# Eight attention groups that load their keys once for two groups

## The chip, the cores and the metric

The kernel runs on one core of one Trainium2 chip. The metric is the device time of a run in microseconds (us), taken as the median of three runs. Five engines work side by side, each through its own row of instructions in order: TensorE (PE: matrix products, with PEld for the loading of its stationary operand), VectorE (DVE), ScalarE (ACT), GpSimd (POOL) and SyncE (SP, which here issues the DMAs). An instruction that needs another engine's result waits for a semaphore, and everything behind it in the same row waits too.

## The reference

Three stages follow each other, on float32 data. Attention has 4 batches, 8 heads, 576 positions and 64 numbers per head; a position sees itself and the 63 before it:

```python
scores = scale * np.matmul(q, k.transpose(0, 1, 3, 2))
mask = (rel >= 0) & (rel < window)          # window = 64
scores = np.where(mask, scores, -1000000000.0)
attn = np.exp(scores - np.max(scores, axis=-1, keepdims=True))
attn = attn / (np.sum(attn, axis=-1, keepdims=True) + 1e-09)
return np.matmul(attn, v)
```

Its output, 2304 rows of 512, goes through `softplus(x @ w_in) @ w_out` (512 to 2048 to 512), and that through `(sigmoid(x @ w_gate) * (x @ w_val)) @ w_out` (512 to 1536 to 512). The result is 2304 x 512.

## The kernel before, in words

**Groups.** Attention is cut into 36 groups of 64 query positions, nine to a batch (`NSEQ`). One group does all 8 heads as 4 pairs (`NPAIR`). Its queries stand block-diagonally, so that one product gives two heads: 128 rows of queries (two heads of 64) against the keys of that pair. The window makes a group need two blocks of 64 keys, its own and the one before; the first group of a batch needs only its own. The input `qk[g]` holds for each group the queries (`qk[g, :, 0]`, 256 KB) and both key blocks (`qk[g, :, 1]`, 256 KB), so each key block lies in memory twice, once for each group that uses it.

**The lead-in.** The tokens of the first big product are cut into blocks (`BLOCKS1`), the first of 512 tokens. That block needs eight groups (`NG0`, groups 0 to 7), and these are worked off before anything else, in the stretch that this document calls the lead-in. Later groups are computed between the products and are not touched by the change. A group of the lead-in goes through these steps, one function each:

- `qk_load`, `v_load` (SP): its queries and keys, its values.
- `att_scores` (PE, L286 and L289): a product of an identity with a mask opens the PSUM bank, then four products, one for each pair of heads, add the scores to it.
- `att_max` (DVE, L299): the maximum of each row. `att_exp` (ACT, L314 and L316): one small scaling, then four exponentials that also sum up their rows. `att_sum` (DVE, L322 and L325): adds the sums and takes the reciprocal. `att_norm` (POOL, L330): multiplies by it.
- `att_transpose` (PE, L338), `att_copy` (DVE or ACT, L367), `att_values` (PE, L376): the probabilities are turned, copied out of PSUM and multiplied with the values.
- `att_hi` (ACT, L384) and `att_lo` (DVE, L389): the result is split into a high and a low part and stored in `xt`, the input of the first big product.

The scores of group g go to the PSUM bank `acc0`, `acc1` or `h1` by g modulo 3. Beside this, the first weights are unpacked (`w_scale` on ACT, L160, then DVE, L179 and L187).

**The start of the main part.** The first big product (`m1_proj(0, 0)`, L394 to L396) waits for the last `att_lo` and for its weights. In front of it stand 21 products on a constant tile (`warm`, L406), which belong to no result. Six more of these open the program. From that product on PE works without long breaks to the end.

**Order.** The order of the lead-in isn't written out. A function `lead_in` plans it: each step has a due time, an engine, an assumed duration and the steps that it waits for (`traits`), and the planner takes the steps one by one by these. An `att_scores` of the lead-in is assumed to take 1.2 us on PE, a `qk_load` is a transfer of 512 KB. What it decides is the order on each engine; the chip then runs this order, whatever the real durations are.

Of the kernel before, what the change touches and what calls it, by code (L numbers as in the profile page):

```python
# [9 lines left out]
F32 = mybir.dt.float32  # L10
# [9 lines left out]
P = 128  # L20
# [21 lines left out]
def tile_kernel(ctx: ExitStack, tc: tile.TileContext, qk, vt, w1, w2, wg, wv, wo, out):  # L42
# [20 lines left out]
    nc = tc.nc  # L63
# [3 lines left out]
    Q = P // 2  # L67
# [48 lines left out]
    def pair(slot, turn, dtype, *shape):  # L116
        key = slot // 2, turn
        if key not in pair_t:
            pair_t[key] = wpool.tile([P, 2, *shape], dtype, tag=f"w{slot // 2}", name=f"w{slot // 2}", bufs=1)
        return pair_t[key]  # L120
# [147 lines left out]

    def qk_load(g):
        if g < NG0:  # L270
            t = pair(NSLOT - NG0 + g, -1, F32, 2, NPAIR, P)[:, g % 2]
        else:
            t = late["apool"].tile([P, 2, NPAIR, P], F32, tag="qk", name="qk", bufs=2)
        nc.sync.dma_start(out=t, in_=qk[g])
        qk_t[g] = t

    def near_bank(g):
# [3 lines left out]
    def att_scores(g):  # L281
        w = width(g)
        t = qk_t[g]
        s = psum(near_bank(g), 1, (P, NPAIR, P)) if g < NG0 else psum("at", 2, (P, NPAIR, P))
        if g < NG0:
            nc.tensor.matmul(out=s[:, :, :w], lhsT=ident16,  # L286
                             rhs=mask16[:, P - w:].unsqueeze(1).to_broadcast([P, NPAIR, w]), start=True, stop=False)
        for j in range(NPAIR):
            nc.tensor.matmul(out=s[:, j, :w], lhsT=t[:, 0, j, :], rhs=t[:, 1, j, :w], start=g >= NG0,  # L289
                             stop=g >= NG0 or j == NPAIR - 1)  # L290
        s_t[g] = s

    def att_max(g):
# [490 lines left out]
    def traits(fn, a, *rest):  # L784
# [3 lines left out]
        if fn is w_load:  # L788
            freed, deps, f = (w_low, a), [], (a - NSLOT) // 2
            if a >= WO_AT:  # L790
                freed, deps = (w_low, a + 1), [(c_hi, NF2 - 1, "x")]
            elif a >= NSLOT:
                freed, deps = (c_send, f, "v"), [(c_hi, f - 1, "x") if f else (w_load, NSLOT - 1)]
            u = a // 2
            slot = raw_slot(u)
            if slot and 4 <= u < 8:
                deps += [(att_scores, 2 * slot - 24), (att_scores, 2 * slot - 23)]
            elif slot and u >= 8:
                deps += [(w_low, 2 * u - 8)]
            return "sp", 512, deps + [(w_load, a - 1, None)] * (a > 0), [("raw", RB, freed)] * (  # L800
                a % 2 == 0 and slot is None)
        if fn in (qk_load, v_load):
            ring = ("qk", 2, (att_scores, a)) if fn is qk_load else ("v", VB, (att_values, a))
            return "sp", 512 if fn is qk_load else 256, [], [ring] * (not early)
        if fn is att_scores:
            if early:
                return "pe", 1.2, [(qk_load, a)], [(near_bank(a), 1, (att_exp, a))]
            return "pe", 0.9, [(qk_load, a), turned(a - 2)], [("at", 2, (att_max, a))]
        if fn is att_max:
            return "dve", 0.8 if early else 1.42 * wide, [(att_scores, a)], [("st", 4, (att_norm, a))] + [  # L810
# [29 lines left out]
        if fn is w_scale:  # L840
            deps, ring, u = [(w_load, a + k) for k in range(size(a))], [], a // 2
            if 0 < u < 4:
                deps += [(att_copy if u == 1 else att_hi, NG0 - 1)]
            if a == 1:
                deps += [(w_scale, 0), (att_copy, NG0 - 1)]
            elif u < 3:
                ring = [("g", GB, (w_lo, 2 * u + 1))]
            elif 4 <= u < 8:
                deps += [(att_scores, 4 + 2 * (u % 4 // 2)), (att_scores, 5 + 2 * (u % 4 // 2))]
            elif 8 <= u < 14:  # L850
                old = u // 2 * 2 - 4 if u < 12 else 10
                deps += [(w_lo, 2 * old + k) for k in range(4)]
            else:
                last = (c_lo, u - NSLOT // 2, "s4") if NSLOT <= a < WO_AT else (w_lo, a + size(a) - 1)
                ring = [("bits", 1, last)]
            return "act", 0.12 + 0.48 * size(a), deps, ring
# [85 lines left out]
    def lead_in():  # L942
# [29 lines left out]
        while todo:  # L972
            ready, other = [], "soft" if table == "exp" else "exp"
            for n, key in enumerate(todo[:AHEAD]):
                rank, kind, us, _, taken = nodes[key]
                deps = deps_of[key] + [rings[name][-bufs] for name, bufs, _ in taken if len(rings[name]) >= bufs]
                if all(d in done for d in deps + after[key]):
                    begin, best = max([done[d] for d in deps], default=0.0), None
                    if kind == "pe" and key[0] not in (m1_proj, m1_out) and key[1] >= NG0:
                        begin += LATE  # L980
                    for kind, us in kind if kind in CHOICES else ((kind, us),):
                        engine, *need = kind.split()
                        start = max(free[engine], begin)
                        if engine == "pool" or "lock" in need:
                            start = max(start, held["dve" if engine == "pool" else "pool"])
                        if engine == "sp" and len(flying) >= FLYING:
                            start = max(start, flying[-FLYING])
                        if engine == "act" and need and need[0] != table:
                            us += SWITCH
                        if best is None or start + us < best[0] + best[2]:  # L990
                            best = start, kind, us
                    ready.append((best[0], rank + FLIP * (best[1].split()[-1] == other), n, key, *best[1:]))
            soonest = min(r[0] for r in ready)
            start, _, n, key, kind, us = min((r for r in ready if r[0] < soonest + (NEAR if soonest < OPEN else SLACK)), key=lambda r: r[1:])
            engine, *need = kind.split()
            for name, _, freed in nodes[key][4]:
                rings[name].append(freed)
            if engine == "sp":
                free[engine] = start + 0.43
                dma = max(start + 1.3, dma) + us / 400  # L1000
                flying.append(dma + 0.75)
                done[key] = dma + 0.85 + MARGIN
            else:
                free[engine] = start + us
                done[key] = start + us + 0.08
                if engine == "pool" or "lock" in need:
                    held[engine] = start + us
                if engine == "act" and need:
                    table = need[0]
            order.append((start, len(order), key + (engine,) * (nodes[key][1] in CHOICES)))  # L1010
            del todo[n]
# [63 lines left out]
```

## Time and profile before

| what | value |
|---|---|
| median of three runs | 894.87 us (894.82 to 895.06) |
| the profiled execution | 895.09 us |
| its span, first to last instruction | 893.3 us |
| PE busy | 885.0 us, 99% of the span |
| lead-in: start of the first big product | 31.18 us after the span's start |
| traffic | 177.58 MB, on average 199 GB/s |

The span is what the rows of a profile cover; the execution lasts 1.8 us longer than it. In a row of the timeline the first number is the start, the second the time from the start of the first to the end of the last instruction in it. Ends of matrix products are modelled, so the distance from one start to the next says more than the second number. A product in float32 appears as two passes, so four products of a group are "x8". A bracket at a row's end is idle time of the engine ahead of it and what ended it.

### The profile page before, as it was taken

To read this page: it belongs to the slowest core of one execution; us is meant where nothing else is said; L and a number is where in the kernel's file an instruction comes from. 1 tells how busy PE (TensorE), PEld (TensorE's weight loads), DVE (VectorE), ACT (ScalarE), POOL (GpSimd) and SP (SyncE) were. 2 spreads that over 40 slices of the span, in tenths; PEclk is the share of its full clock that TensorE was granted. 3 is DMA by queue.
4 is the path that set the end of the run, shared out by engine and by line. 5 is a ranking of instruction groups with operands and counts; after the bars stand their busy time and mean duration, and the time that the engine had idled before them with its cause. 6 is when DMAs were issued, how large, how long until landed. Compare 5 with 4: busy or idle time off the path is not lost.

```text
span 893.3 us, 13510 instructions
## 1 busy us (share of the span) xinstructions
PE 885.0 (99%) x5035; PEld 797.6 (89%) x5035; DVE 523.8 (59%) x921; ACT 400.0 (45%) x892; POOL 153.8 (17%) x157
## 2 busy tenths in 40 slices
PE   9999999999999999999999999999999999999997
PEld 7788789999999888888889999999999999999996
DVE  4898876556555756455515667668445447444444
ACT  6867857546764755345323333334222125222222
POOL 4001102102110220002001333331111112111110
PEclk9999999999999999999999999999999999999999
DMA  9946346766885764683307565545454445544441
GB/s 349 397 151 210 134 163 210 246 199 226 270 268 205 243 234 165 209 287 130 130 1 256 220 254 203 208 174 216 179 209 159 159 164 209 183 165 165 165 165 72
DMA packets 56210, 177.58 MB, mean 199 GB/s; under 512 B 6096, under 2 KB 21456, under 8 KB 51536
## 3 DMA queue, kind: packets, MB, share of 16 engines
q1 hardware_dynamic: 56000, 176.58, 56.0%
q8 instruction: 40, 0.66, 0.3%
q14 instruction: 26, 0.21, 0.1%
q10 hardware_dynamic: 144, 0.13, 0.0%
HBM read 139.72 MB, written 36.96 MB: 198 GB/s over the span
## 4 chain that ended last, share of the span: by engine, by line
PE 97%; DVE 1%; ACT 1%; POOL 0%; issue 0%; POOLq 0%
PE h L394 17%; PE h L396 17%; PE h L395 17%; PE acc L394 11%; PE acc L395 11%; PE acc L396 11%; PE at L289 3%; PE at L376 2%; PE at L396 2%; PE at L395 2%; PE at L394 2%; PE acc L289 1%; PE h L406 1%; PE acc L338 0%; POOL w L330 0%; PE at L338 0%
## 5 line engine op out<-in xcount | busy, mean ns | idle before, releaser
L512 DVE TENSOR_TENSOR w<-h,w 128x384 f32<-128x384 f32 x216 | 117.0, 556 | 159.7 <-PE h L396 157.0
L394 PE MATMUL h<-w,wc 128*128 128x384 f32 x504 | 169.0, 335 | 0.1
L396 PE MATMUL h<-w,wc 128*128 128x384 f32 x504 | 169.0, 335 | 0.0
L395 PE MATMUL h<-w,wc 128*128 128x384 f32 x504 | 168.8, 335 | 0.0
L524 POOL TENSOR_TENSOR g<-w,g 128x384 fp32r<-128x384 f32 x70 | 74.0, 1057 | 296.7 <-ACT g L517 252.1
L394 PE MATMUL acc<-g,w 128*128 128x512 f32 (+1 forms) x320 | 119.5, 374 | 0.0
L394 PE MATMUL h<-xt,w 128*128 128x512 f32 (+1 forms) x320 | 119.4, 373 | 0.1
L396 PE MATMUL h<-xt,w 128*128 128x512 f32 (+1 forms) x320 | 117.9, 368 | 1.0 <-DVE w L187 1.0
L396 PE MATMUL acc<-g,w 128*128 128x512 f32 (+1 forms) x320 | 117.7, 368 | 0.0
L395 PE MATMUL acc<-g,w 128*128 128x512 f32 (+1 forms) x320 | 117.6, 368 | 0.0
L395 PE MATMUL h<-xt,w 128*128 128x512 f32 (+1 forms) x320 | 117.6, 368 | 0.0
L436 DVE TENSOR_TENSOR g<-h,g 128x512 fp32r<-128x512 f32 (+1 forms) x80 | 50.7, 634 | 84.1 <-ACT g L430 83.8
L394 PEld LDWEIGHTS h<-w,wc 128*128 128x128 f32 x504 | 94.6, 188 | 2.4 <-DVE w L512 0.4
L395 PEld LDWEIGHTS h<-w,wc 128*128 128x128 f32 x504 | 94.6, 188 | 2.0
L396 PEld LDWEIGHTS h<-w,wc 128*128 128x128 f32 x504 | 94.6, 188 | 0.0
L423 ACT ACTIVATE h<-h 128x512 f32<-128x512 f32 (+1 forms) x80 | 43.2, 540 | 108.7 <-PE h L396 108.3
L517 ACT CAST g<-w 128x384 fp32r<-128x384 f32 x72 | 36.9, 513 | 117.5 <-DVE w L512 117.5
L396 PEld LDWEIGHTS h<-xt,w 128*128 128x128 f32 x320 | 60.1, 188 | 9.2 <-DVE w L187 1.7
L394 PEld LDWEIGHTS h<-xt,w 128*128 128x128 f32 x320 | 60.1, 188 | 8.4 <-issue 0.6
L394 PEld LDWEIGHTS acc<-g,w 128*128 128x128 f32 x320 | 60.1, 188 | 8.0
L396 PEld LDWEIGHTS acc<-g,w 128*128 128x128 f32 x320 | 60.1, 188 | 7.6
L330 POOL TENSOR_TENSOR p<-p,st 128x512 f32<-128x512 f32 (+1 forms) x28 | 27.8, 996 | 226.2 <-DVE st L325 165.2
(129 smaller groups left out, 1440.9 us busy)
## 6 DMA issues: line engine op xcount, KB each, us to landing
wc<-wcd SPq DMA_DIRECT2D x36, 1792.0 KB, 7.3
qk<-in_qk SPq DMA_DIRECT2D x28, 512.0 KB, 5.1
wcd<-raw SPq DMA_DIRECT2D x24, 512.0 KB, 3.5
w<-in_w SPq DMA_DIRECT2D x16, 512.0 KB, 9.6
raw<-in_w SPq DMA_DIRECT2D x16, 512.0 KB, 4.6
v<-in_vt SPq DMA_DIRECT2D x25, 256.0 KB, 3.8
raw<-in_wg SPq DMA_DIRECT2D x12, 512.0 KB, 4.6
raw<-in_wv SPq DMA_DIRECT2D x12, 512.0 KB, 6.1
```

The lines of the kernel that those rows point to most:

```text
L289: nc.tensor.matmul(out=s[:, j, :w], lhsT=t[:, 0, j, :], rhs=t[:, 1, j, :w], start=g >= NG0, stop=g >= NG0 or j == NPAIR - 1)
L330: nc.gpsimd.tensor_tensor(out=p[:, :, :w], in0=p[:, :, :w], in1=st[:, 2, :].unsqueeze(2).to_broadcast([P, NPAIR, w]), op=ALU.mult)
L376: nc.tensor.matmul(out=o[h * Q:(h + 1) * Q, j, :], lhsT=v[:w, (2 * j + h) * Q:(2 * j + h + 1) * Q], rhs=pt[:w, h, j], start=True, stop=True)
L394: nc.tensor.matmul(out=o, lhsT=lh, rhs=rh, start=first, stop=False)
L395: nc.tensor.matmul(out=o, lhsT=lh, rhs=rl, start=False, stop=False)
L396: nc.tensor.matmul(out=o, lhsT=ll, rhs=rh, start=False, stop=last)
L406: nc.tensor.matmul(out=idle["out"], lhsT=t[:, 0, :P], rhs=t[:, 1], start=True, stop=True)
L423: nc.scalar.activation(out=t, in_=t, func=AF.Softplus)
L436: nc.vector.tensor_tensor(out=g[:, 1, :n], in0=t, in1=g[:, 0, :n].bitcast(F32), op=ALU.subtract)
L512: nc.vector.tensor_tensor(out=out, in0=a, in1=b, op=op)
L517: nc.scalar.copy(out=g[:, 0, :HALF], in_=t)
L524: eng.tensor_tensor(out=g[:, 1, :HALF], in0=t, in1=g[:, 0, :HALF].bitcast(F32), op=ALU.subtract)
```

## The change

For groups 0 to 7 the keys are loaded once for two groups. The tile that two neighbouring groups share takes the keys of the odd one (`qk[g + 1, :, 1]`: the blocks g and g + 1) and the queries of each. An odd group finds both of its key blocks there. An even group finds its own block there; the block before lies in the tile of the pair before. So its four products over 128 key columns become eight products over 64 columns, with the same stationary operand (the queries) for both of a pair of heads. Group 0 has 64 columns in both versions and stays at four products.

The DMAs of the lead-in for queries and keys thus go from 8 of 512 KB to 12 of 256 KB. In the planner a `qk_load` of an odd group counts 256 KB, one of an even group two issues, and the scores wait for the load of the pair before as well. The assumed 1.2 us of `att_scores` stay as they are.

```diff
     def qk_load(g):
         if g < NG0:
-            t = pair(NSLOT - NG0 + g, -1, F32, 2, NPAIR, P)[:, g % 2]
+            t = pair(NSLOT - NG0 + g, -1, F32, 2, NPAIR, P)
+            if g % 2 == 0:
+                nc.sync.dma_start(out=t[:, 1, 1], in_=qk[g + 1, :, 1])
+            nc.sync.dma_start(out=t[:, g % 2, 0], in_=qk[g, :, 0])
         else:
             t = late["apool"].tile([P, 2, NPAIR, P], F32, tag="qk", name="qk", bufs=2)
-        nc.sync.dma_start(out=t, in_=qk[g])
+            nc.sync.dma_start(out=t, in_=qk[g])
         qk_t[g] = t
...
         for j in range(NPAIR):
-            nc.tensor.matmul(out=s[:, j, :w], lhsT=t[:, 0, j, :], rhs=t[:, 1, j, :w], start=g >= NG0,
-                             stop=g >= NG0 or j == NPAIR - 1)
+            if g >= NG0:
+                nc.tensor.matmul(out=s[:, j, :w], lhsT=t[:, 0, j, :], rhs=t[:, 1, j, :w], start=True, stop=True)
+                continue
+            keys = [(0, w, t, 0)] if g % 2 or not g else [(0, Q, qk_t[g - 1], Q), (Q, P, t, 0)]
+            for c0, c1, kt, k0 in keys:
+                nc.tensor.matmul(out=s[:, j, c0:c1], lhsT=t[:, g % 2, 0, j, :], rhs=kt[:, 1, 1, j, k0:k0 + c1 - c0],
+                                 start=False, stop=j == NPAIR - 1 and c1 == w)
...
-            return "sp", 512 if fn is qk_load else 256, [], [ring] * (not early)
+            return "sp", 512 if fn is qk_load and not (early and a % 2) else 256, [], [ring] * (not early)
         if fn is att_scores:
             if early:
-                return "pe", 1.2, [(qk_load, a)], [(near_bank(a), 1, (att_exp, a))]
+                loads = [(qk_load, b) for b in ((a - 1, a) if a % 2 else (a - 2, a)) if b >= 0]
+                return "pe", 1.2, loads, [(near_bank(a), 1, (att_exp, a))]
...
             if engine == "sp":
-                free[engine] = start + 0.43
+                free[engine] = start + 0.43 * (1 + (key[0] is qk_load and key[1] < NG0 and key[1] % 2 == 0))
```

The rest of the diff names the third group that now reads a pair's tile, where that tile is used again later. With other inputs the planner gives another order. What moves stands in three places.

On DVE, at the start of the lead-in before the change (`st_160`, `st_174` and `st_193` are the statistics of groups 0, 1 and 2; a TENSOR_REDUCE that reads a PSUM bank is a group's maximum, one that reads `early` its sum):

```order
L299 TENSOR_REDUCE st_160<-acc0_152 128x4
L299 TENSOR_REDUCE st_174<-acc1_162 128x4
L322 TENSOR_REDUCE st_160<-early_71 128x4
L325 RECIPROCAL st_160<-st_160 128x4
L299 TENSOR_REDUCE st_193<-h1_176 128x4
```

And the same place now (`st_167`, `st_188` and `st_195` are groups 0, 1 and 2; lines are 8 further down):

```order
L307 TENSOR_REDUCE st_167<-acc0_151 128x4
L307 TENSOR_REDUCE st_188<-acc1_161 128x4
L307 TENSOR_REDUCE st_195<-h1_178 128x4
L330 TENSOR_REDUCE st_167<-early_71 128x4
L333 RECIPROCAL st_167<-st_167 128x4
```

The maximum of group 2 has moved ahead of the sum and reciprocal of group 0.

On ACT, from the high part of group 0 on, before (`st_246` is group 4, a COPY is `att_copy`, here of group 3):

```order
L384 CAST xt_264<-at_230 128x4x64
L314 ACTIVATE st_246<-st_246 128x4
L316 ACTIVATE w10_158,early_71<-acc1_219,st_246 128x128 x4
L384 CAST xt_264<-at_274 128x4x64
L367 COPY pt_311<-acc3_295 128x512
```

And now (`st_261` is group 4; the two copies are those of groups 1 and 2):

```order
L392 CAST xt_273<-at_243 128x4x64
L375 COPY pt_289<-acc3_275 128x512
L375 COPY pt_305<-acc2_283 128x512
L322 ACTIVATE st_261<-st_261 128x4
L324 ACTIVATE w10_170,early_71<-acc1_227,st_261 128x128 x4
L392 CAST xt_273<-at_315 128x4x64
```

The copies of groups 1 and 2, which DVE made before, now stand on ACT, ahead of the exponentials of group 4.

On PE, from the transposition of group 0 to that of group 2, before (`acc1_219` and `h1_256` are the scores of groups 4 and 5, `at` the values, `acc2_209`, `acc3_249` and `acc2_289` the transpositions of groups 0, 1 and 2):

```order
L338 MATMUL acc2_209<-ident_69,w8_139 64x128 x4
L286 LDWEIGHTS early_71
L286 MATMUL acc1_219<-early_71 128x512
L289 MATMUL acc1_219<-w14_143 128x128 x4
L376 MATMUL at_230<-pt_216,w8_139 64x64 x8
L338 MATMUL acc3_249<-ident_69,w8_139 128x128 x4
L286 LDWEIGHTS early_71
L286 MATMUL h1_256<-early_71 128x512
L289 MATMUL h1_256<-w14_143 128x128 x4
L376 MATMUL at_274<-pt_262,w8_139 64x64 x8
L338 MATMUL acc2_289<-ident_69,w9_145 128x128 x4
```

And now, from the last of group 4's split products on (`acc1_227` and `h1_265` are the scores of groups 4 and 5, `acc3_275` and `acc2_283` the transpositions of groups 1 and 2):

```order
L297 MATMUL acc1_227<-w13_138,w14_145 128x64
L297 MATMUL acc1_227<-w14_145 128x64
L384 MATMUL at_243<-pt_237,w8_141 64x64 x8
L289 LDWEIGHTS early_71
L289 MATMUL h1_265<-early_71 128x512
L297 MATMUL h1_265<-w14_145 128x128 x4
L346 MATMUL acc3_275<-ident_69,w8_141 128x128 x4
L346 MATMUL acc2_283<-ident_69,w9_148 128x128 x4
```

The scores of group 5 have moved ahead of the transposition of group 1. The first two rows stand four times in a row for group 4, once for each pair of heads.

## Rows read from the trace of the kernel before

**Rows 1.** The page's part 4: the chain that ended last, by engine.

```profile
PE 97%; DVE 1%; ACT 1%; POOL 0%; issue 0%; POOLq 0%
```

**Rows 2.** Timeline of PE in the lead-in: start, length, line, operation, count.

```profile
4.73 1.97 PE L289 MATMUL acc<-w 128*128 128x64 f32 x8
...
6.92 1.91 PE L289 MATMUL acc<-w 128*128 128x128 f32 x8
8.63 0.63 PE L286 MATMUL h<-early 128*128 128x512 bf16 x1
9.05 1.67 PE L289 MATMUL h<-w 128*128 128x128 f32 x8
10.56 0.38 PE L286 MATMUL acc<-early 128*128 128x512 bf16 x1
...
11.67 0.60 PE L338 MATMUL acc<-ident,w 128*64 128x128 f32 x4
...
21.47 0.69 PE L376 MATMUL at<-pt,w 128*64 128x64 f32 x16
22.09 0.66 PE L338 MATMUL acc<-ident,w 128*128 128x128 f32 x4
22.58 1.03 PE L406 MATMUL h<-idle 128*128 128x512 bf16 x4
...
28.27 2.76 PE L406 MATMUL h<-idle 128*128 128x512 bf16 x12
31.18 0.47 PE L394 MATMUL h<-xt,w 128*128 128x512 f32 x1
```

**Rows 3.** Groups of instructions, shapes apart, 36.6 to 38.6 us: busy, mean ns.

```profile
L289 PE MATMUL at<-qk 128*128 128x128 f32 x8 | 1.1, 274 | 0.0
...
L289 PE MATMUL at<-qk 128*128 128x64 f32 x8 | 1.0, 268 | 0.0
```

**Rows 4.** Timeline of DVE in the lead-in.

```profile
8.87 0.69 DVE L299 TENSOR_REDUCE st<-acc 128x4 f32<-128x512 f32 x1 [1.71 <-PE acc L289]
9.48 0.15 DVE L322 TENSOR_REDUCE st<-early 128x4 f32<-128x8 f32 x1
...
10.76 0.69 DVE L299 TENSOR_REDUCE st<-h 128x4 f32<-128x512 f32 x1 [0.92 <-PE h L289]
```

**Rows 5.** Timeline of POOL in the lead-in: the normalisation of group 0.

```profile
10.02 0.61 POOL L330 TENSOR_TENSOR w<-w,st 128x256 f32<-128x256 f32 x1 [5.15 <-DVE st L325]
```

**Rows 6.** Timeline of ACT in the lead-in.

```profile
15.24 0.38 ACT L384 CAST xt<-at 128x256 fp32r<-128x256 f32 x1
15.49 0.24 ACT L314 ACTIVATE st<-st 128x4 f32<-128x4 f32 x1
15.76 0.37 ACT L316 ACTIVATE w<-acc,st 128x128 f32<-128x128 f32 x1
...
17.15 0.38 ACT L384 CAST xt<-at 128x256 fp32r<-128x256 f32 x1
...
20.47 0.59 ACT L367 COPY pt<-acc 128x512 f32<-128x512 f32 x1
20.96 0.21 ACT L314 ACTIVATE st<-st 128x4 f32<-128x4 f32 x1
...
23.11 0.37 ACT L316 ACTIVATE w<-acc,st 128x128 f32<-128x128 f32 x1
...
24.75 0.70 ACT L160 ACTIVATE bits<-w 128x512 f32<-128x512 f32 x1
```

**Rows 7.** Busy time by stretches of 2 us; the last three numbers: clock, DMA, GB/s.

```profile
4.00:6.00 2.00, 2.00 (x9) 1.42 (x8) 0.00 (x0) 0.00 (x0) 0.76 (x3) 1.00 1.02 412
```

**Rows 8.** DMA issues: count, KB each, median us to landing.

```profile
w<-in_qk SPq DMA_DIRECT2D x8, 512.0 KB, 7.0
```

**Rows 9.** Waits, 0 to 45 us: total us, times, longest.

```profile
PEld acc L289 <- DMA w<-in_qk: 0.5, 1, 0.5
```

**Rows 10.** Waits of PE, 60 to 100 us.

```profile
PE h L396 <- DVE w L187: 1.0, 1, 1.0
```

More of the change, by code (lines that the diff above doesn't have):

```diff
@@ L796, in traits @@
             if slot and 4 <= u < 8:
-                deps += [(att_scores, 2 * slot - 24), (att_scores, 2 * slot - 23)]
+                deps += [(att_scores, 2 * slot - 24 + k) for k in range(3)]
             elif slot and u >= 8:
@@ L848, in traits @@
             elif 4 <= u < 8:
-                deps += [(att_scores, 4 + 2 * (u % 4 // 2)), (att_scores, 5 + 2 * (u % 4 // 2))]
+                deps += [(att_scores, min(4 + 2 * (u % 4 // 2) + k, NG0 - 1)) for k in range(3)]
             elif 8 <= u < 14:
```

## The prediction

> **What bounds the kernel now.** I read the chain of waits first. It lies on PE for 97% of the span [rows 1], so a time comes out of this kernel only through PE: by fewer passes, or by an earlier start of them. Then the waits of PE behind the lead-in: one of 1.0 us, for weights from DVE, is the longest [rows 10], so whatever delays the first big product delays the end by as much. That product starts at 31.18 us [rows 2]. The change lies wholly ahead of it, and the question is where this start goes.
>
> So I read the lead-in engine by engine. On PE the reader is to look at the distances between starts [rows 2]. The eight passes of group 1's scores take 8.63 - 6.92 = 1.71 us, 0.214 each. Group 3, opened at 10.56, takes 1.11 us to the transposition at 11.67, of which the opening product is 0.23 (12 products of that width in 2.76 us), so a pass takes 0.11. The opening product of group 2 took 0.42 (8.63 to 9.05). TensorE thus runs at its lower level, 1.2 GHz, at first and at 2.4 GHz later, though the column of the granted clock reads 1.00 already at 4 to 6 us [rows 7]; I go by the durations. Group 2 shows when it rises: its passes take 10.56 - 9.05 = 1.51 us, which is 6 at 0.214 and 2 at 0.11, so at about 10.3 us, after the sixth.
>
> The DMAs move 412 GB/s in 4 to 6 us [rows 7], in 8 loads of 512 KB for queries and keys [rows 8]. But PE waits for such a load once, 0.5 us, at the first score [rows 9]. And the first step of the weights on ACT, at 24.75, carries no wait: it stands behind the exponentials of group 7, not behind its DMA [rows 6]. The keys are not what the lead-in waits for.
>
> **The loads.** 8 x 512 KB become 12 x 256 KB: 1 MB less, at 412 GB/s 2.5 us of DMA time. I cost this at nothing. Ahead of the first score stand 256 KB of keys and 256 KB of queries, as many bytes as before. The work that hides the rest is the lead-in's own chain. The four more issues on SP stand ahead of loads that nobody waits for in these rows. Bounds: the 0.5 us wait goes (-0.5), or the second issue makes the first score as much later again (+0.5). I take 0, by the equal bytes.
>
> **The split passes.** Groups 2, 4 and 6 go from 4 products to 8, so from 8 passes to 16, each over 64 columns instead of 128. If a pass over half the columns took half the time this would be free; if it takes as long, a group costs 8 x 0.11 = 0.88 us more. The trace has both widths with the same 128 x 128 stationary operand, at the higher clock: 8 passes over 128 columns are busy for 1.1 us (274 ns each), 8 over 64 columns for 1.0 us (268 ns) [rows 3]. At the lower clock the same: 1.97 us for group 0's 8 passes over 64 columns, 1.91 for group 1's over 128 [rows 2]. I take the full price.
>
> The Trainium skill speaks on both sides here, in "TensorE: Matmul & The Clock Gate". Its section "Back-to-back issue gap" gives about 60 cycles for up to 64 columns and 134 for 128; by that the split would be nearly free. Its section "LDWEIGHTS (loading the stationary operand)" has the load go by the columns of the stationary operand, whatever is streamed; by that twice the products cost twice. The equal durations of the two widths above bear out the second.
>
> **The path through the changed order.** I follow the first late step to the start of the big product; ends are rounded to a tenth.
>
> 1. PE: group 2 starts its passes at 9.05 as before: 6 at 0.214 and 10 at 0.11 are 2.4 us, to 11.4 instead of 10.56. This is +0.9.
> 2. DVE: the maximum of group 2 follows 0.2 later (10.56 to 10.76 before), at 11.6. The sum of group 0, which started at 9.48, now stands behind it: the maximum occupies 0.61 (8.87 to 9.48), so the sum starts at 12.2. The normalisation on POOL follows the sum by 0.54 (9.48 to 10.02) and takes 0.61: 12.8 to 13.4 instead of 10.02 to 10.63 [rows 4, 5].
> 3. PE: group 3 ends at 11.4 + 1.1 = 12.5, and PE waits until 13.4 for that normalisation; the transposition of group 0 was at 11.67 and held by nothing. Then in the new order: transposition 0.49 (22.09 to 22.58) to 13.9; group 4 with 0.23 + 16 x 0.11 = 2.0 to 15.9; values of group 0 with 0.62 (21.47 to 22.09) to 16.5; group 5 with 1.1 to 17.6; transpositions of groups 1 and 2 to 18.6; group 6 with 2.0 to 20.6; values of groups 1 and 2 to 21.8; then transposition of group 3.
> 4. ACT: the copies of groups 1 and 2 now stand ahead of group 4's exponentials. The first waits for the transposition that starts at 17.6 and ends 0.6 later (0.60 to 0.66 in the rows). Two copies at 0.49 (20.47 to 20.96) end at 19.2, the scaling takes 0.27 (15.49 to 15.76), and the exponentials of group 4 start at 19.5 instead of 15.76: +3.7. The maximum of group 4, done by 16.7, is long there; it is the order on ACT that holds them.
> 5. ACT on: the copy of group 3 waits for the transposition from 21.8 to 22.4 and ends at 22.9; group 5's exponentials start at 23.2. Each further group costs 1.39 of exponentials (15.76 to 17.15), 0.25 of high part (15.24 to 15.49) and 0.27: group 6 at 25.1, group 7 at 27.0, instead of 23.11 [rows 6]. This is +3.9.
> 6. From group 7's exponentials to the first big product it was 31.18 - 23.11 = 8.07 us, over the sum, normalisation, transposition, copy, values and the 12 constant products at 28.27. The same steps stand there in the new order, with 13 constant products: +0.2.
>
> Sum: 3.9 + 0.2 = +4.1, so the first big product starts at about 35.3 us. Behind it the instructions of DVE, ACT and POOL keep their order and start as much later as PE does; the scores of groups 8 and 9 move between the first big products, at equal work. So nothing is won back there. The profiled execution took 895.09 us (span 893.3 and 1.8 around it); 895.09 + 4.1 = 899.2. The median of the three runs lies 0.2 below that execution, so the forecast is 899.0 us. Rounding, the +-0.5 of the loads and a queue of two normalisations on POOL give this case 898.1 to 899.8.
>
> **Rivals.** By 0.2% of the time, 1.8 us, I call two kernels the same; the border of slower lies at 896.7, that of faster at 893.1.
>
> - *The clock rises later.* Before the rise at 10.3 PE did passes over 128 columns (groups 1 and 2); group 0's passes over 64 were followed by more slow ones [rows 2]. Now PE is in passes over 64 columns from 9.05 on, and the rise may come after them. If all of group 2 runs slowly, it ends at 9.05 + 16 x 0.214 = 12.5, 1.0 later, group 3 takes 2.1 instead of 1.1, and the transposition of group 0 comes at 14.6 instead of 13.4: 900.2. If group 4 is slow as well, 16 x 0.104 and 0.2 more: 902.0. For it: other passes stand ahead of the rise than before; against it: PE is without a break in both, and what made it rise is not shown.
> - *A split pass costs half*, as the gap table above has it. Then groups 2, 4 and 6 are each 0.9 shorter, all three on the path: 4.1 - 2.6 = 1.5, so 896.4 us, within the border; only the order remains as a cost. Against it stand the two pairs of rows above, for it only that no row has two products with one stationary operand in succession over half the columns each.
> - *The slack absorbs it.* PE has 21 constant products in the lead-in, some 4.8 us. If the added passes only replaced them, the time would be 894.9 with either sign small. Against it: their number is fixed, and 13 of them still stand behind the last values.
> - *Faster: the loads were the limit after all.* Its place is the first score and the weights. If the first score loses its 0.5 us wait, the weights, 2.5 us earlier, take away the 1.0 us wait behind the lead-in [rows 10], and the rest of the lead-in, which the order lets follow earlier scores, draws in by another 0.5, it is 2.0 us: 892.9. It decides if the passes are free and the new order follows the data without a wait. Against it: one wait for keys in the whole lead-in, and a wait for weights that names DVE, not a DMA.
>
> **How the numbers follow.** Forecast 0.52, later clock 0.24, half price 0.13, absorbed 0.06, faster 0.05. The first two are slower by over 0.2%: 0.76. Half price and absorbed are the same: 0.19. Faster: 0.05. The range reaches down to 896.0, to hold the half price, and up to 901.6, to hold most of the late clock; left out are the absorbed and the faster case and the slowest clock, under 0.2. Predicted is the likeliest, 899.0.
>
> **What would show it.** Right: 16 passes in each of groups 2, 4 and 6 at the spacing of the 8; the sum of group 0 on DVE at 12 us and its normalisation on POOL near 12.8; PE idle for about a microsecond ahead of the first transposition; group 4's exponentials near 19.5; the first big product near 35.3, and the distance from there to the end as before. Wrong: split passes at half the spacing; a start of the big product below 33; a first fast product only after 12 us (the later clock); or a lead-in that comes out late while the end does not, which would mean that time is won back behind it.

## The result and the profile after

The changed kernel takes 899.5 us, median of 6 runs (897.65 to 900.77), against 894.9 before (894.77 to 895.06): a ratio of 1.0051, 95% interval 1.0041 to 1.006. Slower by 0.5%, as forecast (899.0, range 896.0 to 901.6). Five more runs of the same kernel later gave 898.35 (897.59 to 899.79), 1.0038 (1.0025 to 1.0051). Its runs thus spread over 3 us, those of the kernel before over less than 2. That spread is half of the story below. One run of the kernel before (1782.48 us) and one of e3 (3900.55 us) were slow throughout and are left out of every range and ratio here.

The profiled execution of the changed kernel is its longest: 900.77 us, span 899.0. PE in the lead-in (start, length, line, operation; compare [rows 2]):

```profile
4.93 1.08 PE L297 MATMUL acc<-w 128*128 128x64 f32 x8
...
7.45 1.36 PE L297 MATMUL acc<-w 128*128 128x128 f32 x8 [1.23 <-DMA w<-in_qk]
8.60 0.63 PE L289 MATMUL h<-early 128*128 128x512 bf16 x1
9.03 0.58 PE L297 MATMUL h<-w,w 128*128 128x64 f32 x2
...
12.38 0.63 PE L289 MATMUL acc<-early 128*128 128x512 bf16 x1
...
14.52 0.89 PE L346 MATMUL acc<-ident,w 128*64 128x128 f32 x4
...
36.55 0.47 PE L402 MATMUL h<-xt,w 128*128 128x512 f32 x1
```

Group 2 (from 9.03) now has 16 passes, up to the opening of group 3 at 12.38: 3.35 us, 0.21 each. The first big product starts at 36.55 instead of 31.18, 5.37 later; the execution is 900.77 - 895.09 = 5.68 longer. From that start to the end of the execution it is 864.2 us, before it was 863.9. Nothing is won back behind the lead-in, and the wait there is the same one [rows 10]:

```profile
PE h L404 <- DVE w L187: 1.0, 1, 1.0
```

The clock of this execution, by stretches (PE, PEld, DVE, ACT, POOL busy; then granted clock, DMA share, GB/s; compare [rows 7]):

```profile
5.00:8.00 3.00, 1.77 (x14) 1.44 (x14) 0.42 (x1) 1.41 (x9) 0.00 (x0) 1.00 0.90 276
9.00:15.00 6.00, 6.00 (x29) 5.82 (x29) 1.71 (x5) 3.33 (x18) 0.61 (x1) 0.50 1.04 382
15.00:17.00 2.00, 2.00 (x19) 1.95 (x17) 1.60 (x6) 1.58 (x10) 0.45 (x1) 0.98 1.04 385
```

PE was at the higher level (2.4 GHz) for group 0, stood still 1.23 us for the queries of group 1, and ran groups 2 and 3 at the lower one (1.2 GHz, granted clock 0.50). The engines behind it, DVE [rows 4], POOL [rows 5] and ACT [rows 6]:

```profile
12.63 0.69 DVE L307 TENSOR_REDUCE st<-h 128x4 f32<-128x512 f32 x1 [3.09 <-PE h L297]
13.23 0.15 DVE L330 TENSOR_REDUCE st<-early 128x4 f32<-128x8 f32 x1
```
```profile
13.78 0.61 POOL L338 TENSOR_TENSOR w<-w,st 128x256 f32<-128x256 f32 x1 [8.91 <-DVE st L333]
```
```profile
19.65 1.07 ACT L375 COPY pt<-acc 128x512 f32<-128x512 f32 x2 [1.27 <-PE acc L346]
20.86 0.37 ACT L324 ACTIVATE w<-acc,st 128x128 f32<-128x128 f32 x1
...
28.24 0.37 ACT L324 ACTIVATE w<-acc,st 128x128 f32<-128x128 f32 x1
```

The sum of group 0 stands behind the maximum of group 2, its normalisation is 3.8 us late, and on ACT the copies of groups 1 and 2 come just ahead of group 4's exponentials (20.86 instead of 15.76). This is the chain of the forecast.

The loads (DMA issues; compare [rows 8]), and the packets of the first 20 us, in the kernel before and after it:

```profile
w<-in_qk SPq DMA_DIRECT2D x12, 256.0 KB, 5.6
```
```profile
DMA packets 2419, 6.86 MB, mean 343 GB/s; under 512 B 270, under 2 KB 270, under 8 KB 2418
```
```profile
DMA packets 3161, 6.40 MB, mean 320 GB/s; under 512 B 351, under 2 KB 351, under 8 KB 3161
```

A row of queries and keys came in one piece of 4 KB, now in two of 2 KB: more packets, and a lower rate. So the changed kernel is not ahead by its full megabyte.

### The profile page after: what moved, and what is told of

It is laid out like the page before. It is cut to its first block, busy times and chain, and to the rows that moved or that the text cites. A ratio compares the mean times of both kernels' runs of the same rounds, so it can differ in the third digit from the quotient of the medians.

```text
span 899.0 us, 13561 instructions
## 1 busy us (share of the span) xinstructions
PE 888.6 (99%) x5057; PEld 800.4 (89%) x5059; DVE 523.2 (58%) x920; ACT 400.3 (45%) x893; POOL 153.6 (17%) x157
## 4 chain that ended last, share of the span: by engine, by line
PE 97%; DMA 1%; DVE 1%; ACT 1%; issue 0%; POOL 0%; SPq 0%; POOLq 0%
PE h L402 17%; PE h L404 17%; PE h L403 17%; PE acc L402 11%; PE acc L404 11%; PE acc L403 11%; PE at L293 3%; PE at L384 2%; PE at L404 2%; PE at L403 2%; PE at L402 2%; PE acc L297 1%; DMA w<-in_qk 1%; PE acc L346 0%; PE h L297 0%; PE h L414 0%
## 5 line engine op out<-in xcount | busy, mean ns | idle before, releaser
L404 PEld LDWEIGHTS h<-xt,w 128*128 128x128 f32 x320 | 60.0, 188 | 9.0 <-DVE w L187 1.4
L402 PEld LDWEIGHTS h<-xt,w 128*128 128x128 f32 x320 | 60.1, 188 | 8.3 <-issue 0.6
L403 PEld LDWEIGHTS h<-xt,w 128*128 128x128 f32 x320 | 60.1, 188 | 7.3
```

Source lines behind the costliest of these rows:

```text
L402: nc.tensor.matmul(out=o, lhsT=lh, rhs=rh, start=first, stop=False)
L403: nc.tensor.matmul(out=o, lhsT=lh, rhs=rl, start=False, stop=False)
L404: nc.tensor.matmul(out=o, lhsT=ll, rhs=rh, start=False, stop=last)
```

## The experiments

Three edits can be told apart: the loads, the split products, and the planner's table, which sets the order. Six kernels carry them singly and in pairs, and both ends were run again. A ratio is against runs of the kernel before that were taken alongside. "Start" is that of the first big product in the profiled execution, and the last column the rest of that execution.

| loads | split | order | run | median us (range) | ratio, 95% interval | start | rest |
|---|---|---|---|---|---|---|---|
| old | no | old | before; second profile | 895.0 | 1 | 31.18; 29.79 | 863.9; 865.0 |
| old | no | new | e1 | 896.36 (895.86 to 896.93) | 1.0013, 1.0004 to 1.0022 | 31.10 | 865.7 |
| old | yes | old | e2 | 895.79 (895.55 to 896.38) | 1.0009, 1.0001 to 1.0018 | 32.16 | 864.1 |
| new | no | old | e3 | 894.70 (893.56 to 895.55) | 0.9994, 0.9985 to 1.0003 | 29.67 | 863.9 |
| old | yes | new | e5 | 898.22 (897.36 to 898.71) | 1.0033, 1.0021 to 1.0046 | 34.01 | 864.7 |
| new | yes | old | e6 | 896.56 (895.60 to 897.64) | 1.0019, 1.001 to 1.0028 | 32.64 | 863.9 |
| new | no | new | e7 | 897.06 (896.49 to 898.28) | 1.0024, 1.0014 to 1.0034 | 32.20 | 864.4 |
| new | yes | new | after; e8 | 899.5; 898.35 | 1.0051; 1.0038 | 36.55; 34.17 | 864.2; 864.2 |

### The two ends again: e9 and e8

Both kernels without an edit.

> The kernel before, profiled a second time, to see where its clock rises. In the first profile its passes took 0.21 us up to about 10.3 us and the first big product started at 31.18. If the moment of the rise differs from execution to execution in this kernel as well, the second profile shows another one, somewhere from 5 to 10 us, and a start of the big product between 29.5 and 31.2. If the old loading keeps the clock low, it is at 10.3 again and the start within 0.2 of 31.18. Time 894.5 to 895.5 either way.

One execution, 894.79 us. The first profile of before had this opening of group 1:

```profile
6.49 0.63 PE L286 MATMUL acc<-early 128*128 128x512 bf16 x1
```

Now PE and, last, ACT:

```profile
4.73 1.25 PE L289 MATMUL acc<-w 128*128 128x64 f32 x8
5.82 0.38 PE L286 MATMUL acc<-early 128*128 128x512 bf16 x1
...
7.31 1.16 PE L289 MATMUL h<-w 128*128 128x128 f32 x8
8.30 0.38 PE L286 MATMUL acc<-early 128*128 128x512 bf16 x1
...
29.79 0.47 PE L394 MATMUL h<-xt,w 128*128 128x512 f32 x1
...
37.93 0.50 PE L394 MATMUL h<-xt,w 128*128 128x512 f32 x1 [0.47 <-ACT w L179]
```
```profile
30.71 1.14 ACT L160 ACTIVATE bits<-w 128x1024 f32<-128x1024 f32 x1 [0.62 <-DMA w<-in_w]
```

Here the clock rose at about 5 us, not at 10.3: group 0's eight passes take 1.09 us (4.73 to 5.82), where the first profile has 1.76 (4.73 to 6.49, the next opening product). The first big product starts 1.39 earlier than in the first profile, but the execution is only 0.30 shorter. The reader is to see where the rest goes: ACT waits 0.62 us for a weight's DMA at 30.71, and PE 0.47 us for a weight at 37.93; neither wait is in the first profile. In the kernel before, an earlier lead-in runs into the weights. This is why its time hardly shows the clock.

> The changed kernel once more, for its spread and a second profile. My theory: a median of 899.5 us within 0.5 again; in a profile in which group 1 doesn't wait 1.2 us for its queries and the clock is high from 10 us on, the first big product starts near 35.3 us and the time is near 899. Rival (wait and clock carry the cost): without the wait and the low clock the time is near 896 to 897.

Measured 898.35 us, below the 899.0 to 900.0 that was expected and far above the rival's 897; profile 898.35, with a start of 34.17 where 35.3 was expected. In this execution the clock is high from group 0 on (PE, then DVE, POOL and ACT):

```profile
6.69 1.16 PE L297 MATMUL acc<-w 128*128 128x128 f32 x8 [0.41 <-DMA w<-in_qk]
...
8.54 0.43 PE L297 MATMUL h<-w,w 128*128 128x64 f32 x2 [0.48 <-DMA w<-in_qk]
...
10.38 0.38 PE L289 MATMUL acc<-early 128*128 128x512 bf16 x1
...
12.40 0.63 PE L346 MATMUL acc<-ident,w 128*64 128x128 f32 x4 [0.75 <-POOL w L338]
...
34.17 0.47 PE L402 MATMUL h<-xt,w 128*128 128x512 f32 x1
```
```profile
11.19 0.15 DVE L330 TENSOR_REDUCE st<-early 128x4 f32<-128x8 f32 x1
```
```profile
11.73 0.61 POOL L338 TENSOR_TENSOR w<-w,st 128x256 f32<-128x256 f32 x1 [6.84 <-DVE st L333]
```
```profile
18.48 0.37 ACT L324 ACTIVATE w<-acc,st 128x128 f32<-128x128 f32 x1
```

16 passes in 1.84 us (8.54 to 10.38), where e9 takes 0.99 for 8 (7.31 to 8.30). A split group costs 0.85 us, and PE waits 0.75 us ahead of the first transposition. With the clock early in both, the start moves from 29.79 to 34.17, +4.38. The difference between the two profiled executions of the changed kernel, 900.77 and 898.35, is 2.42 us, and their starts differ by 2.38. The passes of group 2 alone are 1.51 of it (3.35 against 1.84), so this is mainly the clock.

### One edit alone: e1, e2, e3

e1, the order: before, with the planner's table of the change (one line of it, shortened).

```diff
-            return "sp", 512 if fn is qk_load else 256, ...
+            return "sp", 512 if fn is qk_load and not (early and a % 2) else 256, ...
```

> The kernel before, whole loads and whole products, but worked off in the order that the planner makes for the changed kernel. My theory (passes 2.6 us, order 1.5 us, loads nothing): the order alone costs 1.5 us, 896.4 us, and the normalisation of group 0 on POOL starts at about 12 us instead of 10. Rival (the time comes from the loads that land late and from the clock that falls then): no cost, 894.9 us within 0.3, and PE has no wait for keys beyond the 0.5 us of before.

896.36 us, as expected. But the normalisation of group 0 starts at 9.89 us, not near 12: the clock is high from about 5 us on here. Part of the time is a wait that neither end has: the new order also moves the scores of group 8, and they stand ahead of the arrival of their load. The rest is 865.7.

```profile
31.10 0.47 PE L397 MATMUL h<-xt,w 128*128 128x512 f32 x1
...
34.95 1.16 PE L290 MATMUL at<-qk 128*128 128x128 f32 x8 [0.86 <-DMA qk<-in_qk]
```

e2, the split: before, with each even group's four products cut into eight on the old tile.

```diff
-            nc.tensor.matmul(out=s[:, j, :w], lhsT=t[:, 0, j, :], rhs=t[:, 1, j, :w], ...)
+            for c0, c1 in [(0, w)] if g % 2 or not g else [(0, Q), (Q, P)]:
+                nc.tensor.matmul(out=s[:, j, c0:c1], lhsT=t[:, 0, j, :], rhs=t[:, 1, j, c0:c1], ...)
```

> The kernel before with its loads and its order; only the scores of groups 2, 4 and 6 are split into products over 64 columns, from the group's own tile. My theory: each split group takes 0.9 us longer on PE (up to 1.7 where the clock is at 1.2 GHz), together 2.6 us, of which most lies on the path: 896.5 to 897.7 us. Rival (half the columns, half the time, or PE has slack): 894.9 us within 0.3. If the passes over 64 columns also put off the rise of the clock, over 898 us, and group 3 shows passes at 0.21 us.

895.79 us, less than the 896.5 to 897.7 that was expected and above the 895.2 up to which the rival went. In the old order three times 0.85 us on PE costs 0.7 in the median. In that order the normalisation of group 0 doesn't stand behind group 2's scores, and, if e9 is a guide, the weights hide the first microsecond.

```profile
32.16 0.47 PE L398 MATMUL h<-xt,w 128*128 128x512 f32 x1
```

e3, the loads: the shared tile, one product per pair of heads for every group, old order.

```diff
+            nc.tensor.matmul(out=s[:, j, :w], lhsT=t[:, g % 2, 0, j, :], rhs=t[:, 1, 1, j, :w], ...)
```

> The shared loads of the changed kernel (12 of 256 KB) in the order of before, with whole products: an even group reads both key blocks of its own pair's tile, which are the wrong keys for groups 2, 4 and 6, at equal work. My theory as forecast: the loads cost nothing, 894.9 us within 0.5. Rival (seen in the profile of the changed kernel: group 1's scores waited 1.2 us for their queries, and the granted clock was 0.50 for some 6 us after it): the same wait shows here, the clock falls after it, and the time is 1 to 3 us above before, 896 to 898, with a spread over the runs of more than 1 us.

894.70 us, as expected. The profiled execution took 893.56, the shortest of all kernels:

```profile
29.67 0.47 PE L400 MATMUL h<-xt,w 128*128 128x512 f32 x1
```

It starts like the second profile of before (29.79) and ends 1.23 us earlier, without those two waits: three weights are unpacked on ACT in a row from 27.75 us, where e9 stood before the third. In this execution the weights come earlier. But it doesn't show in the median beyond the uncertainty.

### Two edits: e5, e6, e7

e5 is split and order on the old loads, e6 loads and split in the old order, e7 loads and order without the split; the edits are those above.

> Split products and the new order, with the whole loads of before. The order alone cost 1.3 us and the split alone 0.7. My theory now: in the order of before the split passes lay beside other waits, in the new order the scores of groups 4 and 6 stand ahead of transpositions that everything waits for, so all three times 0.9 us come onto the path: 1.3 + 2.6, 899.0 us within 0.6, nearly all of the change. Rival (the rest of the change comes from the loads): the sum of the two, 897.1 us within 0.5.

> The shared loads and the split products of the changed kernel, right in their result, in the order of before. My theory: as with the split alone, 0.7 us above before with the loads at -0.4 to 0: 895.5 us within 0.6. Rival (small loads that land late, and passes over 64 columns at a clock that falls in the wait): over 897 us, with PE waiting for queries at group 1 or 2 and granted clock of 0.50 in some stretch before 15 us.

> The shared loads and the new order with whole products; groups 2, 4 and 6 read the wrong keys, both blocks of their own pair's tile. My theory: the order's 1.3 us and the loads' -0.4: 896.0 us within 0.6. Rival (loads and order together make group 1 wait and the clock fall): 897.5 us or more, with a spread of over 2 us.

898.22, 896.56 and 897.06 us. None lies where it was expected: e5 is 0.2 below its band and 0.6 above the rival's; e6 and e7 are 0.5 above theirs and half a microsecond below the rival's. Each pair costs more than its two edits alone: 3.3 us against 2.0 (e5), 1.6 against 0.3 (e6), 2.1 against 0.9 (e7), always some 1.2 more. That fits a slack of about a microsecond that hides a part of every edit made alone, as e9 shows one in the kernel before (1.39 us of start, 0.30 of time).

```profile
34.01 0.47 PE L398 MATMUL h<-xt,w 128*128 128x512 f32 x1
```
```profile
32.64 0.47 PE L402 MATMUL h<-xt,w 128*128 128x512 f32 x1
```
```profile
32.20 0.47 PE L400 MATMUL h<-xt,w 128*128 128x512 f32 x1
```

e5 has the old loads and starts within 0.16 us of e8: passes and order alone make most of the change (3.3 us in the median, against 3.4 for e8 and 4.6 for the first six runs of the changed kernel). From the column of starts, with 29.79 for before, each edit can be priced four times. The split costs 2.37 (e2 - before), 2.91 (e5 - e1), 2.97 (e6 - e3) and 1.97 (e8 - e7), on average 2.56. The order costs 1.31, 1.85, 2.53 and 1.53, on average 1.8. The loads cost -0.12, 0.48, 1.10 and 0.16, on average 0.4. These are single executions whose clocks rise at different moments (in e2 only at about 7.5 us), so a price is good to some 0.6 us. In the medians, each against its runs of the kernel before, the same four differences give 0.7 to 2.0 for the split (on average 1.5), 1.3 to 2.6 for the order (2.0) and -0.4 to 0.9 for the loads (0.4). In time the split is thus worth less than in the start, and the order about as much as the split or more.

### A planner that knows the price: e4

```diff
-                return "pe", 1.2, loads, [(near_bank(a), 1, (att_exp, a))]
+                return "pe", 1.2 + 0.9 * (a > 0 and a % 2 == 0), loads, [(near_bank(a), 1, (att_exp, a))]
```

> The changed kernel with one number of the planner changed: the scores of groups 2, 4 and 6 are assumed to take 2.1 us on PE instead of 1.2, so the order follows the real durations. My theory: the order's 1.5 us mostly go, 897.5 us, against 899.5 for the changed kernel; the sum of group 0 stands ahead of the maximum of group 2 again and the first big product starts near 34 us. Rival (loads and clock carry the cost): within 0.5 us of the changed kernel, 899 to 900, with its wait for keys and its spread.

897.69 us (895.64 to 901.74; 12 runs), ratio 1.0028 (1.0018 to 1.0038); its profiled execution took 896.2:

```profile
32.34 0.47 PE L402 MATMUL h<-xt,w 128*128 128x512 f32 x1
```

The time is the expected one, and the sum of group 0 stands ahead of the maximum of group 2 again (8.46 and 10.56 us). Told of the 16 passes, the planner finds an order that starts 1.8 us earlier than e8, about as the old order does (e6); 34 was expected. Against the first six runs of the changed kernel (1.0041 to 1.0060) the gain is clear; against e8 (1.0025 to 1.0051) the intervals overlap, so its size, 0.7 to 1.8 us in the median, is not sure.

### Keeping PE busy ahead of group 1: e10

```diff
+        if g == 0:
+            for _ in range(5):
+                warm()
```

> The changed kernel with five more products on the constant tile behind the scores of group 0, where PE otherwise stands still for the queries of group 1 (1.23 us in the first profile of the changed kernel, 0.41 in the second). They take 1.1 us at the higher clock. If that standstill is what lets the clock fall behind group 1, as in the first profile, the clock now stays high, the passes from group 2 on take 0.11 in every execution, the first big product starts at 34.2 to 34.7, the time is 898.2 to 898.9 and the runs lie within 1.2 us of each other. If the clock falls for another reason, the spread stays at 2 to 3 us, up to 900 and above.

900.37 us (898.49 to 901.07), ratio 1.0054 (1.0041 to 1.0067): neither shorter nor steadier, the second case of the expectation. PE has no break here, and its passes were slow in the profiled execution all the same:

```profile
6.78 2.34 PE L417 MATMUL h<-idle 128*128 128x512 bf16 x5
8.92 0.63 PE L289 MATMUL acc<-early 128*128 128x512 bf16 x1
9.34 1.64 PE L297 MATMUL acc<-w 128*128 128x128 f32 x8
...
36.56 0.47 PE L405 MATMUL h<-xt,w 128*128 128x512 f32 x1
```
```profile
5.00:10.00 5.00, 4.95 (x18) 3.51 (x19) 0.42 (x1) 1.50 (x9) 0.00 (x0) 1.00 0.90 276
```

The five products took 2.1 us (6.78 to 8.92), not 1.1. But this execution is not one in which the clock fell: it had not risen yet. That comes within group 1, at about 10.5 us by the spacing of the passes. At the lower level the five products themselves put group 1's scores back to 9.34, from 7.45 and 6.69 in the two profiles of the changed kernel. So e10 shows that filling doesn't make the clock high in every execution; whether the standstill brings the clock down, it doesn't test. The next run speaks against that.

### Sharing without a split: e11, e12

The even group gets its 64 old keys by one more DMA into the free quarter of its tile, and one product reads both blocks. e12 has the five products of e10 as well.

```diff
+                if g:
+                    nc.sync.dma_start(out=t[:, 0, 1, :, :Q], in_=qk[g, :, 1, :, :Q])
...
+            keys = t[:, 1, 1, j, :w] if g % 2 or not g else t[:, :, 1, j, :Q]
```

> The keys are still loaded once for two groups, but an even group gets its block of 64 keys from the pair before by one more DMA of 128 KB, into the free quarter of its own tile, laid so that one product reads both blocks with a stride: eight passes as before, and the order of the kernel before. If the cost of the change was the passes and the order, nothing of it is left: 894.4 to 895.3, start of the first big product 29.7 to 31.3. If the sharing itself costs (more and smaller DMAs, a strided read of the keys), 896 to 897.

> As the kernel of three such DMAs and the old order, and five products on the constant tile behind the scores of group 0. If a clock that is high from the first groups on in every execution is worth what the passes of groups 0 to 2 say (16 passes by 0.1 us, 1.6 us, less what then waits for a load), 893.2 to 894.2, faster than both kernels. If the lead-in's end hangs on something else than these passes (loads, or ACT), or the five products only push the scores back, 894.8 to 896.

896.02 us (894.94 to 896.82), ratio 1.0009 (1.0000 to 1.0018), and 895.90 (894.78 to 896.67), 1.001 (1.0001 to 1.002). Neither beats the kernel before. e11, PE and the clock:

```profile
8.76 1.13 PE L298 MATMUL h<-w 128*128 128x128 f32 x8 [1.45 <-DMA w<-in_qk]
...
12.49 1.13 PE L298 MATMUL acc<-w 128*128 128x128 f32 x8 [0.84 <-DMA w<-in_qk]
...
31.24 0.47 PE L403 MATMUL h<-xt,w 128*128 128x512 f32 x1
```
```profile
9.00:15.00 6.00, 5.16 (x53) 4.53 (x53) 3.30 (x9) 4.56 (x25) 2.34 (x3) 1.00 1.09 355
```

Split and order are gone, and the start, 31.24, is within what the first case of the expectation gave; the time is that of the second. PE now waits 1.45 and 0.84 us for loads of groups 2 and 4. This way of sharing costs a microsecond, and what it has more than e3, which cost nothing, is three loads in pieces of 256 bytes (in the first 20 us 1914 packets under 512 bytes, against 351 in the changed kernel) and the strided read. The read isn't slower (eight passes take 1.13 us, as those of group 2 in e3 do), so it is likely the loads; it was not tried apart. And the clock stayed at 1.00 behind a standstill of 1.45 us, longer than the 1.23 of the first profile of the changed kernel. In e12 the first products were already at the higher level, so the fill bought nothing:

```profile
6.03 1.24 PE L418 MATMUL h<-idle 128*128 128x512 bf16 x5
...
9.38 1.13 PE L298 MATMUL h<-w 128*128 128x128 f32 x8 [0.79 <-DMA w<-in_qk]
```

## Why the prediction was right, step by step

| step | forecast | e8, clock early | first profile after, clock low from 8 to 15 us |
|---|---|---|---|
| end of group 2's passes | 11.4 | 10.38 | 12.38 |
| maximum of group 2, sum of group 0 (DVE) | 11.6, 12.2 | 10.58, 11.19 | 12.63, 13.23 |
| normalisation of group 0 (POOL) | 12.8 | 11.73 | 13.78 |
| first transposition (PE) | 13.4, held by POOL | 12.40, held 0.75 | 14.52, behind group 3 |
| exponentials of group 4 (ACT) | 19.5 | 18.48 | 20.86 |
| exponentials of group 7 | 27.0 | 25.86 | 28.24 |
| first big product | 35.3 | 34.17 | 36.55 |

**The chain** came as written. From the end of group 2 to the first big product the forecast has 23.9 us; e8 has 23.8 and the first profile 24.2. What is off is the first row, by -1.0 or +1.0. In e8 the clock is early, and waits for loads (0.41 and 0.48 us) give a part of that back. In the first profile group 2 starts at 9.03, nearly the forecast's 9.05, but from a fast group 0 and a wait of 1.23 us; then its passes are slow to the end, at a granted clock of 0.50. I had taken a rise at 10.3 us from one profile as a property of the kernel; it is one of the execution. The forecast lies between the two cases, and a median over runs of both kinds could meet it. That part of the hit, 899.0 against 899.5 and then 898.35, is luck; the chain from group 2 on is not.

**The split passes** at the full price: forecast 0.88 us a group, measured 0.85; 2.6 on the start, measured 2.56 on average. In the median time it is 1.5. The rival that a split pass costs half is out: the spacing is 0.115 us, that of passes twice as wide.

**The order**: 1.5 left over in the forecast, about 1.8 measured on the start and 2.0 in the time.

**The loads**: costed at nothing, with half a microsecond either way, on the grounds that as many bytes stand ahead of the first score. The first score was the wrong place to look at alone: it came only 0.2 to 0.3 us later (4.93 and 4.99 instead of 4.73). PE meets the loads at groups 1 and 2 (0.41 and 0.48 us in e8, 1.23 in the first profile). With an early clock PE waits for whole loads too (0.38 and 0.58 us in e1, 0.56 in e5, 0.39 in e9). Group 2's passes start at 7.31 to 8.38 us with those (e9, e1, e5) and at 7.80 to 9.02 with the shared ones (e3, e4, e6, e7, e8). So "the keys are not what the lead-in waits for" was true of one execution with a late rise, not of the kernel. As a term the loads measured 0.4 on average, within the bounds, with single prices from -0.12 to 1.10.

**"Whatever delays the first big product delays the end by as much"**: true of the changed kernel, and not of the one before when its lead-in is early. There 1.39 us of start were worth 0.30 of time. So of the 4.38 us that the start moved between e9 and e8, only 898.35 - 894.79 = 3.56 show at the end.

**Rivals.** The later clock has its numbers in the profiled execution: 900.77, within the 900.2 to 902.0 given for it. But it did not come as written. There was no late rise: the clock was high for group 0, fell between 8 and 9 us and rose again at 15. I had it as an alternative to the forecast; it is a companion, and the clock differs within one kernel. Here the Trainium skill bears on it: "TensorE: Matmul & The Clock Gate", section "What's actually happening", says that the number of slow products at the start of one kernel differs from run to run. The two profiles of the kernel before agree, with a rise at about 10.3 and at about 5 us. The slack that absorbs the passes is not there, in the constant products; a smaller one is, in the weights of the kernel before. And the rival that the loads were the limit has something for it in one execution: e3 ends 1.23 us before e9 from nearly the same start, without the waits for weights. Its median doesn't confirm it, and the passes and the order spend more than that.

**Open.** What sets the moment of the clock's rise, and why it fell between 8 and 9 us in one execution: a standstill by itself doesn't bring it down (e11 kept the clock through a longer one), and no run filled the standstill in an execution with an early clock and the changed kernel's loads. Whether each long run of the changed kernel is one of a low clock is likely from two profiles and not shown for runs without one. And whether the lower rate of the loads comes from pieces of 2 KB or from fewer bytes in flight was not separated by a run; e3 speaks for the pieces. From 4 to 6 us its DMA engines are as busy as those of before [rows 7], a share of 1.04 against 1.02, and move 286 GB/s instead of 412:

```profile
4.00:6.00 2.00, 1.90 (x9) 1.14 (x7) 0.00 (x0) 0.00 (x0) 0.75 (x3) 1.00 1.04 286
```

## What to carry to other kernels

Here, cutting a float32 product of 128 columns in two over its columns, with the stationary operand as wide as before, doubled its price; a saving in bytes has to be worth that. A planner with a table of durations should be told the new duration in the same edit: here it put the sum of group 0 behind the maximum of group 2 with the old number, and ahead of it with the new one (e4). And before a start time from one profile is used as a base, it is worth a second profile: an early stretch can differ by microseconds between executions and still end at the same time, because something else hides it.

## What the runs showed of the hardware

- The clock's rise in one and the same program: about 10.3 us in one execution and 5 in another, at 1.4 us of difference in the first big product. By the spacing of the passes the other executions lie from 5 us or earlier (e1, e4, e8, e11, e12) over 6 (e3, e5, e6, e7) and 7.5 (e2) to 10.5 (e10).
- The granted clock reads 1.00 in stretches whose passes take 0.21 us [rows 7], also in e10 from 5 to 10 us, and 0.50 in another execution with the same spacing (9 to 15 us). Spacings of passes are the safer reading.
- The loads ran slower as 256 KB in pieces of 2 KB than as 512 KB in pieces of 4 KB. From 2 to 7 us, in the kernel before and after it (last number GB/s), 351 became 281; the other executions with whole loads have 329 to 352 (e1, e2, e5, e9), those with the shared loads 235 to 290 (e3, e4, e6, e7, e8, e10):

```profile
2.00:7.00 5.00, 5.00 (x17) 3.04 (x18) 0.27 (x2) 0.01 (x1) 2.37 (x9) 1.00 1.00 351
```
```profile
2.00:7.00 5.00, 4.22 (x16) 1.86 (x16) 0.44 (x2) 0.42 (x3) 2.37 (x9) 1.00 0.85 281
```

SP stood 1.7 us before one issue in the changed kernel, waiting for an earlier load:

```profile
SPq L265 <- DMA w<-in_qk: 3.1, 5, 1.7
```
